# Hashing two more head pairs with GpSimd products and VectorE sums instead of TensorE matmuls

## The chip, the core and the metric

The kernel runs on one NeuronCore of a Trainium2 chip. TensorE (PE) multiplies matrices, VectorE (DVE) and ScalarE (ACT) work on tiles, GpSimd (POOL) is a second, slower elementwise engine that cannot read the matmul accumulators (PSUM), and SyncE (SP) has the queue that most transfers are issued from. Every engine works through its own instructions in the order in which they were written; they meet only at semaphores. The metric is the device time of one execution in microseconds.

## The reference

Attention with a hash mask, followed by a gated feed-forward layer. There are 4 batches of 8 heads, 768 tokens, head dimension 64.

```python
q_bits = (einsum('bhsd,dk->bhsk', q, proj) > 0)      # 6 bits for each token
k_bits = (einsum('bhsd,dk->bhsk', k, proj) > 0)
mask   = q_bucket[..., :, None] == k_bucket[..., None, :]
scores = where(mask, scale * q @ k.T, -1e9)
attn   = softmax(scores) @ v                          # [batch, head, token, 64]
x      = attn, heads side by side                     # [3072, 512]
out    = x + sigmoid(x @ w_res) * ((gelu(x @ w_gate) * (x @ w_val)) @ w_out)
```

The kernel does not build a mask. It appends the six bits, as +0.5 or -0.5, to each token's 64 values of q and k (with one constant column), so that the score matmul itself falls far below the others unless all six bits agree.

## The kernel before

Heads are taken in pairs: 16 pairs, 4 in a batch (batch 0 has pairs 0 to 3, batch 1 has 4 to 7, batch 2 has 8 to 11, batch 3 has 12 to 15). For each batch there are two stages.

The attention stage has 36 slots, nine for each pair. A slot is one call of `scores` (L542, two banks of scores, then one exponential on ScalarE, L553) and, two slots behind, one call of `values` (L515, the products with v). Between them `mlp_mm` issues a few steps of the output projection of the batch before (`project`: L598 for the residual gate, L614 for the product with `w_out`, L617 and L621 on VectorE to finish), so that TensorE never runs dry. A counter spreads these steps: `HELD` = 16 of them are kept for the end of the stage, in the last batch `HELD_LAST` = 20. Each head's accumulator `av` is opened by a memset (L482), preset by a small matmul (L490), copied over its token tiles by VectorE (L494), accumulated into, and normalised (L466, L467). The normalised tokens are turned by a transfer (L470) into `x_sb`.

The gate/value stage has 12 steps (`gate_val`): eight matmuls with `w_gate` and eight with `w_val` (L566), GELU on ScalarE (L583), a product on VectorE (L586). The first three quarters of step 0 (`begun`) are issued ahead, while the last pair's tokens are still being turned.

Before a pair can be attended to, its q and its k must each be loaded (L108), cast into one of four `nat` tiles (L223 for q, L225 for k), hashed, its bits written beside the cast values, and the tile turned by a transfer (L372) into `aug`. There are two ways of hashing:

- By TensorE: VectorE transposes the load (`tr`, L265, into one of six `t32` buffers), 16 matmuls take two pairs at once (`hash_mm`, L283), VectorE transposes the result (`hash_tok`, L303) and writes the bits with four instructions for each of q and k (`bits`, L319).
- By GpSimd and VectorE: for each of the six bits GpSimd multiplies the load with one row of the projection, copied to all partitions (`part`, L357, into one of the same six `t32` buffers), VectorE sums over the 64 values (`part_sum`, L361), and one instruction writes the bits (`bits_sum`, L365). The projection rows come by a transfer (`rows`, L349) and are rearranged by GpSimd (`rows_turned`, L353).

The order of all this is written out by hand. `at(s, ...)` puts work behind slot s, `gv(b, m, ...)` behind step m of batch b's gate/value stage. Batch 1's pairs are all hashed by TensorE in batch 0's stages. For batches 2 and 3 the first two pairs (`xs`) are loaded and transposed in the attention stage of the batch before and hashed by TensorE beside gate step 0, and the last two (`ys`) are hashed by products and sums, whose places `PROD` and `SUMS` count steps: 0 to 11 are steps of the gate/value stage, 12 and up are slots of the next attention stage. GpSimd also casts v and sums it (`vals_a` L432, `vals_s` L440 to L444) for each pair.

Of the kernel before, what the change touches and what calls it, by code (L numbers as in the profile page):

```python
# [46 lines left out]
def kernel(  # L47
# [12 lines left out]
    nc = tc.nc  # L60
    B, H, S, D = q.shape
    NBITS = proj.shape[1]
# [4 lines left out]
    KF = DFF // P  # L67
# [37 lines left out]
    def load(p, side, eng=None):  # L105
        b, hp = divmod(p, HP)
        s = ld_pool.tile([P, HT, D], FP32, tag=f"ld{side}", name=f"ld{side}")
        (eng or nc.sync).dma_start(  # L108
            s.rearrange("p (h t) d -> p h (t d)", h=2),
            (q, k)[side][b, 2 * hp:2 * hp + 2].rearrange("h (p t) d -> p h (t d)", t=T))  # L110
        raw[p, side] = s
# [90 lines left out]
    for s in range(3):  # L202
        n = KF // 3
# [57 lines left out]
    def tr(p, side, h0=0, h1=2):  # L261
        if (p, side) not in t32:
            t32[p, side] = t32_pool.tile([P, HT, 2, 32], FP32, tag="t32", name="t32")
        sl = slice(h0 * T, h1 * T)
        nc.vector.transpose(t32[p, side][:, sl].rearrange("p c h n -> p (c h n)"),  # L265
                            raw[p, side][:, sl].rearrange("p c d -> p (c d)"))
# [80 lines left out]
    def rows():  # L347
        pn = o_pool.tile([P, DMODEL], FP32, tag="o", name="pn")[:, 0:D * NBITS]
        nc.sync.dma_start(pn, proj.rearrange("d n -> (d n)").unsqueeze(0).to_broadcast([P, D * NBITS]))  # L349
        return pn  # L350

    def rows_turned(pn):
        nc.gpsimd.tensor_copy(prow, pn.rearrange("p (d n) -> p n d", n=NBITS))  # L353

    def part(x, j):
        pd = t32_pool.tile([P, HT, D], FP32, tag="t32", name="pd")
        nc.gpsimd.tensor_mul(pd, raw[x], prow[:, j].unsqueeze(1).to_broadcast([P, HT, D]))  # L357
        hparts[x, j] = pd

    def part_sum(x, j):  # L360
        nc.vector.tensor_reduce(stripes(hsum6)[:, :, :, j],  # L361
                                hparts.pop((x, j)).rearrange("p (a c) d -> p a c d", a=3), axis=mybir.AxisListType.X, op=ALU.add)

    def bits_sum(x):
        nc.vector.tensor_scalar(nat_of(x)[:, :, D:D + NBITS].rearrange("p (a c) n -> p a c n", a=3),  # L365
                                stripes(hsum6), 0.0, 0.5,
                                op0=ALU.is_gt, op1=ALU.subtract)

    def turn(p, side):
        x = (p, side)  # L370
        ag = aug_pool.tile([P, HT, P], BF16, tag=f"aug{side}", name=f"aug{side}")
        nc.sync.dma_start_transpose(out=ag, in_=nat_of(x).rearrange("p c n -> p (c n)"))  # L372
        aug[x] = ag
# [184 lines left out]
    gv_work = {}  # L558
# [11 lines left out]
    def gate_val(b, begun, beside=None):  # L570
        for m in range(KF):
            ps = []
            for i, w in enumerate((wg, wv)):
                if m == 0:
                    sp = gv_mm(b, m, w, KM - 1, KM, begun[i])
                else:
                    sp = gv_mm(b, m, w, 0, KM)
                ps.append(sp)
                if m == 0 and i == 1 and beside:
                    beside()  # L580
                if w is wg:
                    gt = g_pool.tile([P, S], BF16, tag="gt", name="gt")
                    nc.scalar.activation(gt, sp[:, 0:S], AF.Gelu)  # L583
            if m == 0 and b > 0:
                hidden[b] = hh_pool.tile([P, KF, S], BF16, tag="hh", name="hh")
            nc.vector.tensor_mul(hidden[b][:, m, :], gt, ps[1][:, 0:S])  # L586
            for piece in gv_work.pop((b, m), []):
                piece()
# [70 lines left out]
    NSLOT = HP * NCH  # L659
    LAST = NPAIR * NCH  # L660
    LAG = 2
    HELD = 16
    HELD_LAST = 20
# [3 lines left out]
    def at(s, *pieces):  # L667
        side_work.setdefault(s, []).extend(pieces)
# [4 lines left out]
    def gv(b, m, *pieces):  # L673
        gv_work.setdefault((b, m), []).extend(pieces)

    def loads(s, *xs):
        for p, what in xs:
            if what == "v":
                at(s, lambda p=p: load_v(p))
            elif p >= NPAIR - 2:  # L680
                for hi in range(2):
                    at(s, lambda p=p, w=what, hi=hi: load_head(p, "qk".index(w), hi, nc.sync))
            else:
                at(s, lambda p=p, w=what: load(p, "qk".index(w)))
# [15 lines left out]
    def tokens(ps, psum=False):  # L700
        hash_tok([(p, side) for p in ps for side in range(2)], psum)
# [67 lines left out]
    begun = []  # L769
# [7 lines left out]
    PROD = (0, 0, 0, 0, 0, 1, 2, 2, 6, 7, 8, 8, 10, 10, 10, 12, 13, 13, 13, 19, 19, 20, 22, 27)  # L777
    SUMS = (1, 2, 2, 4, 4, 6, 7, 8, 9, 10, 10, 11, 12, 12, 13, 17, 19, 21, 21, 23, 23, 29, 30, 31)
    CASTS = (2, 5, 10, 11)
    VALS = (9, 6)  # L780
    LAYS = (0, 0, 3, 5)

    def lay(b, m, x):
        gv(b, m, lambda: bits(*x), lambda: turn(*x))

    for b in range(B - 1):
        s0, p0 = b * NSLOT, (b + 1) * HP
        xs = [(p0 + i, side) for i in range(2) for side in range(2)]
        ys = [(p0 + 2 + i, side) for i in range(2) for side in range(2)]
        if b > 0:  # L790
            for j, (x, y) in enumerate(zip(xs, ys)):
                at(s0 + 24 + 2 * j, lambda x=x: tr(*x))
                at(s0 + 25 + 2 * j, lambda x=x: cast(*x, nc.gpsimd))
                loads(s0 + 2 + 4 * j, (x[0], "qk"[x[1]]))
                loads(s0 + 18 + 3 * j, (y[0], "qk"[y[1]]))
            gv(b, 0, lambda p0=p0: tokens((p0, p0 + 1), True))
            for m, x in zip(LAYS, xs):
                lay(b, m, x)
            for m, y in zip(CASTS, ys):
                gv(b, m, lambda y=y: cast(*y, nc.gpsimd))  # L800
        else:
            for m, names in enumerate(BESIDE):
                for name in names.split():
                    gv(b, m, first.pop(name))
        if b >= FROM:
            s1 = s0 + NSLOT

            def put(n, piece):
                if n < 0:
                    at(s1 + n, piece)  # L810
                elif n < KF:
                    gv(b, n, piece)
                else:
                    at(s1 + n - KF, piece)

            plan = []
            for i, (y, j) in enumerate((y, j) for y in ys for j in range(NBITS)):
                plan.append((PROD[i] + .3, lambda y=y, j=j: part(y, j)))
                plan.append((SUMS[i] + .2, lambda y=y, j=j: part_sum(y, j)))
                if j == NBITS - 1:  # L820
                    plan.append((SUMS[i] + .2, lambda y=y: (bits_sum(y), turn(*y))))
            for n, piece in sorted(plan, key=lambda e: e[0]):
                put(int(n // 1), piece)
    for p in range(HP, NPAIR):
# [7 lines left out]
    NMM = T * (KM + KF)  # L832

    def mlp_mm(n):
        while mlp and n > 0:
            try:
                next(mlp[0])
                n -= 1
                done[0] += 1
            except StopIteration:  # L840
                mlp.pop(0)

    pn = []
    gv(0, 9, lambda: pn.append(rows()))
    gv(0, 11, lambda: rows_turned(pn[0]))
    gate_val(0, begun)
    mlp.append(project(0))
    for s in range(NSLOT, LAST):
        p, c = divmod(s, NCH)
        b, slot = divmod(s, NSLOT)  # L850
        cur = scores(p, c)
        for piece in side_pe.pop(s, []):
            piece()
        held_back = (HELD_LAST - HELD) * (b == B - 1) * max(0, slot - 12) // (NSLOT - 1 - 12)
        mlp_mm(AHEAD + (slot + 1) * (NMM - HELD - AHEAD) // NSLOT - held_back - done[0])
        pending.append(cur)
        while len(pending) > LAG:
            values(*pending.pop(0))
        for piece in side_work.pop(s, []):
            piece()  # L860
        if slot == NSLOT - 1:
            values(*pending.pop(0))
            ps = (HP * (b + 1), HP * (b + 1) + 1)
            mlp_mm(4)
            flush()
            begun = [gv_mm(b, 0, w, 0, KM - 1) for w in (wg, wv)]
            if b < B - 1:
                mlp_mm(NMM)
                gate_val(b, begun, lambda: hashed(ps))
            else:  # L870
                mlp_mm(HELD_LAST - 10)
                gv(b, 0, lambda: mlp_mm(NMM))
                gate_val(b, begun, lambda: mlp_mm(3))
            done[0] = 0
            mlp.append(project(b))
    assert not side_pe and not side_work and not gv_work
# [32 lines left out]
```

## Time and profile before

| | |
|---|---|
| Median of 3 runs | 339.99 us (339.33 to 340.06) |
| Profiled execution | 339.88 us, of which the profile's span is 338.2 us |
| TensorE | busy 330.4 us (98%) |
| VectorE | busy 216.2 us (64%) |
| ScalarE | busy 205.8 us (61%) |
| GpSimd | busy 171.7 us (51%) |

The profile is one execution as the chip's profiler recorded it. A row of a timeline gives the start and the length in us, the engine, the line of the kernel, the operation, the tile written and the tiles read, the shape, how many were merged, and in brackets how long the engine sat idle before it and what released it. A row of a tile or line view gives count and shortest/median/longest duration in ns. A row of a table by stretches gives, for a stretch of the span, its length and the busy us (and number of instructions) of TensorE's matmuls, TensorE's weight loads, VectorE, ScalarE and GpSimd, then the granted TensorE clock, the share of the transfer engines in use, and GB/s. A row of waits gives who was waited for, the us in total and the number of times.

### The profile page before, as it was taken

The page shows a single profiled execution, that of the slowest core. Times are in us where ns is not written, and L with a number is a line of the kernel's source. Part 1 is how long each engine was busy: PE and PEld are TensorE (multiplying, and loading weights), DVE is VectorE, ACT ScalarE, POOL GpSimd, SP SyncE. Part 2 cuts the span into 40 slices and gives each one's busy share as a digit, 9 for nine tenths or more (in the row PEclk, how much of TensorE's full clock was granted, in tenths as well). Part 3 has the DMA queues.
Part 4 walks back from the last instruction along what each step waited for, and adds up shares of the span by engine and source line. Part 5 has one row for each costly group of instructions (what it writes and reads, how often), then busy time and mean ns, then how long its engine had stood idle before and what let it go on. Part 6 is the DMA issues. An engine that isn't in the chain of part 4 may idle for free.

```text
span 338.2 us, 7541 instructions
## 1 busy us (share of the span) xinstructions
PE 330.4 (98%) x3005; PEld 202.7 (60%) x3052; DVE 216.2 (64%) x417; ACT 205.8 (61%) x231; POOL 171.7 (51%) x220
## 2 busy tenths in 40 slices
PE   8999999999999999999999999999999999999995
PEld 4667766555666665665666665666566665666444
DVE  5889457657344847878897765887897434343343
ACT  3899962327999962225999982233999984223220
POOL 6877920801657105998999703998998000000000
PEclk9999999999999999999999999999999999999999
DMA  7989999997985733550487832551251432000012
GB/s 228 378 136 266 215 198 175 175 167 126 209 193 159 237 101 77 95 96 0 105 223 219 251 113 75 96 105 34 48 141 45 99 56 56 31 0 2 31 62 96
DMA packets 72323, 43.29 MB, mean 128 GB/s; under 512 B 50400, under 2 KB 69344, under 8 KB 72288
## 3 DMA queue, kind: packets, MB, share of 16 engines
q1 hardware_dynamic: 65872, 37.56, 43.9%
q0 software_dynamic: 6336, 5.24, 10.5%
q8 instruction: 24, 0.39, 0.5%
q14 instruction: 11, 0.09, 0.1%
q10 hardware_dynamic: 80, 0.00, 0.0%
HBM read 29.56 MB, written 6.29 MB: 106 GB/s over the span
## 4 chain that ended last, share of the span: by engine, by line
PE 95%; DVE 2%; issue 1%; ACT 0%; DVEq 0%
PE sp L566 36%; PE sp L542 19%; PE fps L614 18%; PE av L515 10%; PE rps L598 6%; PE hs L283 2%; PE pt L384 2%; PE wps L189 1%; PE hs L330 1%; DVE hh L586 1%; DVE o L621 1%; DVE fps L617 0%; PE av L487 0%; DVE nat L319 0%; DVE hs L336 0%
## 5 line engine op out<-in xcount | busy, mean ns | idle before, releaser
L553 ACT ACTIVATE e<-sp 128x1024 bf16<-128x1024 f32 x108 | 108.7, 1028 | 7.8 <-PE sp L542 2.8
L357 POOL TENSOR_TENSOR pd<-ld,prow 128x768 f32<-128x768 f32 x48 | 86.1, 1817 | 38.3 <-PE hs L283 34.8
L583 ACT ACTIVATE gt<-sp 128x768 bf16<-128x768 f32 x48 | 38.9, 810 | 89.2 <-PE sp L566 89.2
L542 PE MATMUL sp<-aug,aug 71*128 71x256 bf16 (+1 forms) x384 | 85.8, 325 | 0.0
L614 PE MATMUL fps<-wo,hh 128*128 128x512 bf16 (+2 forms) x289 | 75.0, 361 | 1.3
L586 DVE TENSOR_TENSOR hh<-gt,sp 128x768 bf16<-128x768 bf16 x48 | 45.8, 954 | 40.8 <-PE sp L566 35.1
L566 PE MATMUL sp<-x_sb,wv 128*128 128x256 bf16 (+1 forms) x376 | 70.5, 325 | 0.6 <-DVE hh L586 0.2
L566 PE MATMUL sp<-x_sb,wg 128*128 128x256 bf16 (+1 forms) x376 | 70.5, 325 | 0.5
L515 PEld LDWEIGHTS <-e 128*128 128x128 bf16 x864 | 40.2, 97 | 25.0
L566 PEld LDWEIGHTS <-wv 128*128 128x128 bf16 x384 | 37.5, 98 | 25.1 <-issue 0.4
L566 PEld LDWEIGHTS <-wg 128*128 128x128 bf16 x384 | 37.0, 98 | 25.7 <-issue 1.5
L361 DVE TENSOR_REDUCE hsum<-pd 128x12 f32<-128x768 f32 x48 | 44.2, 942 | 0.4
L515 PE MATMUL av<-va,e 128*128 128x65 bf16 x864 | 43.4, 193 | 0.1
L614 PEld LDWEIGHTS <-hh 128*128 128x128 bf16 x312 | 28.3, 97 | 22.0
L553 ACT ACTIVATE hh<-sp 128x1024 bf16<-128x1024 f32 x36 | 34.7, 1026 | 3.2 <-PE sp L542 2.9
L542 PEld LDWEIGHTS <-aug 71*128 71x128 bf16 x384 | 29.2, 97 | 10.4 <-issue 1.1
L617 DVE SCALAR_TENSOR_TENSOR fps<-th,fps 128x512 f32<-128x512 f32 (+2 forms) x26 | 16.9, 649 | 25.6 <-PE fps L614 25.1
L602 ACT ACTIVATE th<-rps 128x512 f32<-128x512 f32 x24 | 14.3, 594 | 21.3 <-PE rps L598 21.3
L494 DVE COPY av<-av 128x390 f32<-128x390 f32 x24 | 13.7, 571 | 19.0 <-PE av L490 19.0
L598 PE MATMUL rps<-wr,x_sb 128*128 128x512 bf16 x88 | 25.2, 378 | 0.3
L265 DVE STREAM_TRANSPOSE t<-ld 128x768 f32<-128x768 f32 (+1 forms) x24 | 22.1, 926 | 0.1
L223 POOL TENSOR_SCALAR nat<-ld 128x768 bf16<-128x768 f32 (+1 forms) x16 | 13.0, 815 | 16.3 <-issue 15.7
(77 smaller groups left out, 258.9 us busy)
## 6 DMA issues: line engine op xcount, KB each, us to landing
ldv<-in_v_dram SPq DMA_DIRECT2D x16, 384.0 KB, 4.7
out_dram<-o SPq DMA_DIRECT2D x23, 256.0 KB, 2.2
ld<-in_q_dram SPq DMA_DIRECT2D x13, 384.0 KB, 4.6
ld<-in_k_dram SPq DMA_DIRECT2D x13, 384.0 KB, 5.4
wg<-in_moe_w_gate_dram POOLq DMA_DIRECT2D x4, 384.0 KB, 6.7
wv<-in_moe_w_val_dram POOLq DMA_DIRECT2D x4, 384.0 KB, 8.4
wo<-in_moe_w_out_dram POOLq DMA_DIRECT2D x3, 512.0 KB, 8.1
ld<-in_q_dram SPq DMA_DIRECT2D x6, 192.0 KB, 4.5
```

The costliest lines, as they stand in the source:

```text
L265: nc.vector.transpose(t32[p, side][:, sl].rearrange("p c h n -> p (c h n)"), raw[p, side][:, sl].rearrange("p c d -> p (c d)"))
L357: nc.gpsimd.tensor_mul(pd, raw[x], prow[:, j].unsqueeze(1).to_broadcast([P, HT, D]))
L361: nc.vector.tensor_reduce(stripes(hsum6)[:, :, :, j], hparts.pop((x, j)).rearrange("p (a c) d -> p a c d", a=3), axis=mybir.AxisListType.X ...
L515: nc.tensor.matmul(av[p, hi][:, qt, :], e[:, off:off + P], va[:, hi, jt, 0:D + 1], start=first, stop=(p >= HP and jt == T - 1), skip_group ...
L542: nc.tensor.matmul(sp[:, off:off + nq * P], ks[0:KA, hi * T + jt, :], qs[0:KA, hi * T + qt0:hi * T + qt0 + nq, :], start=True, stop=True)
L553: nc.scalar.activation(e, sp, AF.Exp, scale=float(ALPHA))
L566: nc.tensor.matmul(sp[:, c0:c1], w[:, kk, bass.ts(m, P)], xs[:, kk, c0:c1], start=(kk == 0), stop=(kk == KM - 1))
L583: nc.scalar.activation(gt, sp[:, 0:S], AF.Gelu)
L586: nc.vector.tensor_mul(hidden[b][:, m, :], gt, ps[1][:, 0:S])
L598: nc.tensor.matmul(rps, x_sb[b][:, kk, t, :], wr[:, kk, :], start=(kk == 0), stop=(kk == KM - 1))
L614: nc.tensor.matmul(fps[:, cs], hh[:, m, bass.ts(t, P)], wo[:, m, cs], start=(m == 0), stop=(m == KF - 1))
L617: nc.vector.scalar_tensor_tensor(fps[:, cs], th[:, cs], 1.0, fps[:, cs], op0=ALU.add, op1=ALU.mult)
```

## The change

A constant `EARLY = 1` names the batch whose attention stage prepares batch 2. For it alone, all four pairs of batch 2 are hashed by products and sums:

- The `tr` transposes, `hash_mm`, `hash_tok` and `bits` of pairs 8 and 9 are left out.
- Their loads, casts, products and sums get places of their own, counted back from the end of batch 1's attention: -1 to -36 are its slots, -37 and below are steps of batch 0's gate/value stage. The first load and products stand in that stage, most of the rest in the attention stage, the last three sums in steps 1 to 3 of batch 1's gate/value stage.
- Pairs 10 and 11 get a new list of places (`PROD1`, `SUMS1`), later than `PROD` and `SUMS`.
- `rows` and `rows_turned` move from steps 9 and 11 of batch 0's gate/value stage to steps 2 and 4.
- Batch 1 takes over batch 3's way of holding 20 projection steps back and issuing them around gate step 0, where the hash matmuls stood.

```diff
+    EARLY = 1
+    XLOADS = (-45, -42, -38, -28)
+    XCASTS = (-34, -31, -17, 0)
+    XPROD = (-43, -41, -39, -36, -36, -36, -36, -30, -29, -24, -24, -23, -21, -21, -19, -18, -16, -16, -14, -10, -6, -3, -3, -3)
+    XSUMS = (-40, -40, -34, -33, -31, -28, -23, -23, -22, -21, -19, -19, -16, -14, -10, -10, -10, -9, -4, -3, -3, 1, 2, 3)
+    PROD1 = (-1, 3, 4, 4, 5, 7, 7, 7, 7, 8, 8, 11, 13, 14, 14, 18, 18, 18, 20, 22, 23, 24, 24, 27)
+    SUMS1 = (4, 5, 6, 6, 7, 8, 9, 9, 12, 13, 15, 16, 16, 16, 19, 19, 21, 22, 25, 26, 29, 29, 29, 31)
+    CASTS1 = (3, 3, 4, 10)
...
             for j, (x, y) in enumerate(zip(xs, ys)):
+                loads(s0 + 18 + 3 * j, (y[0], "qk"[y[1]]))
+                if b == EARLY:
+                    continue
                 at(s0 + 24 + 2 * j, lambda x=x: tr(*x))
                 at(s0 + 25 + 2 * j, lambda x=x: cast(*x, nc.gpsimd))
                 loads(s0 + 2 + 4 * j, (x[0], "qk"[x[1]]))
-                loads(s0 + 18 + 3 * j, (y[0], "qk"[y[1]]))
...
             def put(n, piece):
-                if n < 0:
+                if n < -NSLOT:
+                    gv(b - 1, n + NSLOT + KF, piece)
+                elif n < 0:
                     at(s1 + n, piece)
...
+            if b == EARLY:
+                for n, m, x in zip(XLOADS, XCASTS, xs):
+                    put(n, lambda x=x: load(*x))
+                    plan.append((m + .1, lambda x=x: cast(*x, nc.gpsimd)))
+                lot(xs, XPROD, XSUMS)
+                lot(ys, PROD1, SUMS1)
+            else:
+                lot(ys, PROD, SUMS)
...
-    gv(0, 9, lambda: pn.append(rows()))
-    gv(0, 11, lambda: rows_turned(pn[0]))
+    gv(0, 2, lambda: pn.append(rows()))
+    gv(0, 4, lambda: rows_turned(pn[0]))
...
-        held_back = (HELD_LAST - HELD) * (b == B - 1) * max(0, slot - 12) // (NSLOT - 1 - 12)
+        held_back = (HELD_LAST - HELD) * (b in (EARLY, B - 1)) * max(0, slot - 12) // (NSLOT - 1 - 12)
...
-            if b < B - 1:
+            if b in (EARLY, B - 1):
+                mlp_mm(HELD_LAST - 10)
+                gv_work.setdefault((b, 0), []).insert(0, lambda: mlp_mm(NMM))
+                gate_val(b, begun, lambda: mlp_mm(3))
+            else:
                 mlp_mm(NMM)
                 gate_val(b, begun, lambda: hashed(ps))
```

More of the change, by code (lines that the diff above doesn't have):

```diff
@@ L794 @@
                 loads(s0 + 2 + 4 * j, (x[0], "qk"[x[1]]))
-                loads(s0 + 18 + 3 * j, (y[0], "qk"[y[1]]))
[L796 to L799, printed above, removed]
+            if b != EARLY:
+                gv(b, 0, lambda p0=p0: tokens((p0, p0 + 1), True))
+                for m, x in zip(LAYS, xs):
+                    lay(b, m, x)
+            for m, y in zip(CASTS1 if b == EARLY else CASTS, ys):
                 gv(b, m, lambda y=y: cast(*y, nc.gpsimd))
@@ L816, with lot @@
             plan = []
[L817 to L821, printed above, removed]
+            def lot(jobs, prod, sums):
+                for i, (y, j) in enumerate((y, j) for y in jobs for j in range(NBITS)):
+                    plan.append((prod[i] + .3, lambda y=y, j=j: part(y, j)))
+                    plan.append((sums[i] + .2, lambda y=y, j=j: part_sum(y, j)))
+                    if j == NBITS - 1:
+                        plan.append((sums[i] + .2, lambda y=y: (bits_sum(y), turn(*y))))
+            if b == EARLY:
[6 more added lines that the diff above has]
+                lot(ys, PROD, SUMS)
             for n, piece in sorted(plan, key=lambda e: e[0]):
@@ L866 @@
             begun = [gv_mm(b, 0, w, 0, KM - 1) for w in (wg, wv)]
-            if b < B - 1:
+            if b in (EARLY, B - 1):
[3 more added lines that the diff above has]
+            else:
                 mlp_mm(NMM)
                 gate_val(b, begun, lambda: hashed(ps))
[L870 to L873, printed above, removed]
             done[0] = 0
```

## The prediction

> **What bounds the kernel now.** First the page's 40 slices and the chain that ended last, then a table by stage.
>
> ```profile
> POOL 6877920801657105998999703998998000000000
> PE 95%; DVE 2%; issue 1%; ACT 0%; DVEq 0%
> ```
>
> TensorE carries 95% of the chain: what it issues is the time, and another engine costs something only where TensorE comes to wait for it. GpSimd (POOL) has its empty slices around 44 to 107 us, which is where the change puts work.
>
> ```profile
> core 0: us, PE busy (x) PEld busy (x) DVE busy (x) ACT busy (x) POOL busy (x), PEclk, DMA share, GB/s
> 80.50:123.50 43.00, 42.50 (x471) 26.47 (x478) 22.75 (x49) 39.24 (x43) 18.54 (x31) 1.00 0.74 181
> 123.50:158.80 35.30, 35.04 (x236) 20.78 (x238) 25.99 (x45) 11.80 (x15) 26.74 (x18) 1.00 0.37 77
> 158.80:201.70 42.90, 42.40 (x470) 26.46 (x477) 33.60 (x62) 39.28 (x43) 33.11 (x39) 1.00 0.67 178
> 237.00:279.00 42.00, 41.50 (x463) 26.05 (x471) 28.26 (x54) 38.93 (x42) 23.77 (x27) 1.00 0.36 78
> 279.00:313.70 34.70, 34.49 (x212) 20.39 (x213) 13.85 (x17) 11.60 (x14) 0.00 (x0) 1.00 0.07 22
> ```
>
> The rows are attention of batch 1 and its gate/value stage, attention of batch 2, then attention and gate/value stage of batch 3. In each TensorE is busy within 0.5 us of the stage. Batch 1 takes 78.3 us; batch 3, in whose gate/value stage nothing is hashed, takes 76.7. The granted clock is 1.00. VectorE's (DVE's) busy time goes from 22.75 us in the first attention stage to 33.60 in the second, and the stage gets no longer: VectorE has room.
>
> **Part 1: the hash matmuls go.** This is the end of batch 1's attention on TensorE, and the same place in batch 3, whose schedule batch 1 now takes.
>
> ```profile
> 128.76 1.51 PE L283 MATMUL hs<-t,projw 128*32 128x192 f32 x32
> 130.20 1.48 PE L566 MATMUL sp<-x_sb,wg 128*128 128x512 bf16 x8
> ```
>
> From 128.76 to 130.20 TensorE does nothing but the hash: 1.44 us, in line with nothing beside it. The build has 16 such matmuls fewer (two records each). The stage table prices the same thing a second way: 78.3 - 76.7 = 1.6 us. I take 1.44, the row of the thing itself. The held-back output projection (20 steps instead of 16 left for the gate/value stage) only moves TensorE work: its four steps leave attention (43.0 to about 42.1) and come back behind gate step 0. ScalarE then has 39.2 us in 42.1; batch 3 does 38.93 in 42.0, so that costs nothing.
>
> **Part 2: work taken off and put on VectorE and GpSimd.**
>
> ```profile
> 130.49 0.59 DVE L303 STREAM_TRANSPOSE htp<-hs 128x384 f32<-128x384 f32 x1
> 131.11 1.91 DVE L319 TENSOR_SCALAR nat<-htp 32x72 bf16<-32x72 f32 x8
> L265 DVE STREAM_TRANSPOSE t<-ld 128x768 f32<-128x768 f32 x4 | 3.8, 955 | 0.0
> L361 DVE TENSOR_REDUCE hsum<-pd x48: 896/945/956, 134.0 to 260.7; 128x12 f32<-128x768 f32 x48
> 160.93 0.23 DVE L365 TENSOR_SCALAR nat<-hsum 128x72 bf16<-128x72 f32 x1
> L357 POOL TENSOR_TENSOR pd<-ld,prow x48: 1804/1817/1834, 107.9 to 256.5; 128x768 f32<-128x768 f32 x48
> 130.33 7.12 POOL L357 TENSOR_TENSOR pd<-ld,prow 128x768 f32<-128x768 f32 x4 [18.81 <-PE hs L283]
> ```
>
> Off VectorE: 4 transposes 3.8, one token transpose 0.59, 16 bit writes 2 x 1.91; 8.2 us. Onto it: 24 sums x 0.945 + 4 x 0.23 = 23.6 us. Onto GpSimd: 24 products, back to back 7.12 / 4 = 1.78 each, 42.7 us. In the build's order 2 of the new sums stand in gate/value stage 0, 19 in attention 1 and 3 in stage 1; of the later 24 (pairs 10, 11), 8 stand in stage 1 and 16 in attention 2. Attention 1 then has 22.75 - 3.8 + 19 x 0.945 + 3 x 0.23 = 37.6 us of VectorE in 42.1. None of it is TensorE's, so it is priced at nothing as long as three covers hold.
>
> **Cover A: the eviction copies.** Each head's accumulator is preset by TensorE, copied by VectorE (L494), then accumulated into two steps later for a pair's first head, one step later for its second. Sums queued ahead of the copy delay it.
>
> ```profile
> 98.03 0.56 DVE L494 COPY av<-av 128x390 f32<-128x390 f32 x1
> 99.39 0.56 DVE L467 TENSOR_TENSOR x_tok<-av,rec 128x384 bf16<-128x384 f32 x1
> 101.97 0.57 DVE L494 COPY av<-av 128x390 f32<-128x390 f32 x1 [1.83 <-PE av L490]
> 104.43 0.41 PE L515 MATMUL av<-va,e 128*128 128x65 bf16 x8
> 107.78 0.57 DVE L494 COPY av<-av 128x390 f32<-128x390 f32 x1 [0.64 <-PE av L490]
> 109.12 0.41 PE L515 MATMUL av<-va,e 128*128 128x65 bf16 x8
> ```
>
> The copy at 101.97 may end 1.9 us later (104.43); the one at 107.78, a second head, 0.95 (the second half of the step at 109.12). The worst place in the new order is the first: behind the copy that ends at 98.59 stand a sum (to 99.5), the normalisation (0.8, to 100.3), a sum, a memset and two sums (to 103.2), 0.23, and the copy: it ends at 104.0, with 0.4 us to spare. Of the others in attention 1 none is closer. In attention 2:
>
> ```profile
> 80.50:104.40 23.90, 23.62 (x249) 14.49 (x252) 10.14 (x25) 22.40 (x25) 11.58 (x22) 1.00 0.92 204
> 158.80:182.70 23.90, 23.62 (x250) 14.54 (x253) 20.08 (x37) 22.53 (x25) 23.43 (x26) 1.00 0.67 179
> ```
>
> With VectorE at 20.08 instead of 10.14 us of 23.9, TensorE does the same 23.62. The change adds three sums to the second stretch (16 for 13): 22.9 of 23.9. Bounds for what that costs: nothing (this pair of rows) to 1.0 us (22.9 being full within the 1.0 that is left, and all of that met as one wait). I take 0.1, because the row nearest to it, 84% busy, shows nothing.
>
> **Cover B: GpSimd in time.** A sum whose product is late stops VectorE's queue, evictions included.
>
> ```profile
> 66.41 1.63 POOL L225 CAST nat<-ld 128x768 bf16<-128x768 f32 x2
> 83.50 0.87 POOL L353 COPY prow<-pn 128x384 f32<-128x384 f32 x1 [15.47 <-DMA pn<-in_proj_dram]
> 84.35 0.99 POOL L440 TENSOR_TENSOR v<-ldv 128x384 f32<-128x384 f32 x1
> 87.21 1.00 POOL L440 TENSOR_TENSOR v<-ldv 128x384 f32<-128x384 f32 x1
> 182.68 0.94 DVE L361 TENSOR_REDUCE hsum<-pd 128x12 f32<-128x768 f32 x1
>   POOL pd L357: 3.2, 4
> 71.39 0.95 DVE L586 TENSOR_TENSOR hh<-gt,sp 128x768 bf16<-128x768 bf16 x1 [0.76 <-PE sp L566]
> 58.19 0.84 SPq L116 DMA_DIRECT2D ldv<-in_v_dram  x1
> pn<-in_proj_dram SPq DMA_DIRECT2D x1, 192.0 KB, 4.9
> DMA to landing us min/median/max: 2.6/4.7/9.2
> ```
>
> GpSimd is free of weight loads at 66.41. The projection rows now go into SyncE's queue ahead of the transfer at 58.19; with the 4.9 us that they took to land (the row "pn") they are there by 64, and the first load, issued next, by about 68 if it takes the longest that a q or k load took (9.2 us, the last row). The first two products end near 69 and 71; their sums stand behind the gate product at 71.39, so nothing waits. From there to the last product of pair 11: 0.85 + 48 products x 1.78 + 10 casts x 0.8 + 6 value pairs x 2.86 (84.35 to 87.21) = 111.5 us, to 177.9. Its sum is due at 182.68 - 1.44 = 181.2: 3.3 us free, against 3.2 us that GpSimd waited before for product buffers (the row "POOL pd L357"). So the last product comes about when it is due. In SyncE's queue the row transfer and the first three transfers (0.84 us or so each to issue) pass ahead of the turns of pairs 4 to 7, which are needed from 80.5 on and are some 3 us later for it at 60; in attention 1 the new turns wait there for their bits, with output stores and token turns behind them whose VectorE work stands behind the same bits. Nothing.
>
> **Cover C: the last token turn of batch 1.** Gate step 0's last quarter needs it, and batch 3's schedule leaves less work in front.
>
> ```profile
> 119.96 0.56 DVE L467 TENSOR_TENSOR x_tok<-av,rec 128x384 bf16<-128x384 f32 x1
> 123.68 0.20 DVE L466 RECIPROCAL rec<-av 128x6 f32<-128x6 f32 x1
> 279.46 0.56 DVE L467 TENSOR_TENSOR x_tok<-av,rec 128x384 bf16<-128x384 f32 x1
> 283.14 0.49 PE L566 MATMUL sp<-x_sb,wg 128*128 128x512 bf16 x2
> DMA to landing us min/median/max: 2.7/2.9/5.2
> ```
>
> 280.02 + 2.9 = 282.9, so 0.2 us is left in batch 3, and in batch 1 a memset, two sums and a copy, 0.11 + 1.89 + 0.57 = 2.6 us, now stand between the last two normalisations, where 123.68 - 120.52 = 3.2 us lie (3.0 in the shortened stage): they fit. Cost nothing, up to 1 us if the product there is late.
>
> **The sum.** -1.44 + 0.1 = -1.3 on the profiled execution: its span 338.2 becomes 336.9 and its 339.88 us 338.5; the median of the runs, 339.99, lies 0.1 above it: 338.6.
>
> **Rivals.**
> 1. Late products (slower). Buffer waits double with the number of products: 6.4 instead of 3.2, so the last product comes 3.1 us late, and the copies behind its sum have 0.95 of slack: TensorE waits 2.2 us, 340.8. It decides from 1.44 + 0.95 = 2.4 us of lateness on. For it: 3.3 us of room is little over 115. Against: the long waits of before (18.81 us in the row of part 2) were for hash matmuls, not for sums. Chance 0.22.
> 2. The gain is eaten: several small waits at covers A and C, together 0.8 to 2.1 us, leave 339.3 to 340.6. For it: margins of 0.2 and 0.4 us. Against: the 84% row. Chance 0.18.
> 3. Products and sums shut each other out. The 48 products last 1804 to 1834 ns with sums running beside most of them, a spread of 30 ns, so this hardly happens. If each new product lost half a sum, 24 x 0.47 = 11 us, GpSimd would be some 11 us late and the time near 349. Chance 0.02. The Trainium skill, Perfetto Trace Analysis, Optimizing Scalar/DVE Operations, warns that moving work between GpSimd and VectorE might not help since they share an SBUF read port; by that warning this rival is the outcome, but the trace's 30 ns disagree for reductions.
>
> **How the numbers follow.** Forecast 0.58. 0.2% is 0.68 us, about what runs can tell from no change. Forecast and a little of rival 2 make faster 0.60; the rest of 2 and the mildest of 1, 0.16 within 0.2%; 0.24 slower. The likeliest case alone reaches from 338.2 (1.6 and no waits, less 0.2 of scatter) to 339.2; the range goes up to rival 1's time with a little scatter: 338.2 to 341.0.
>
> **What would show it.** Right: no hash between steps 0 and 1 of stage 1, batch 1 at 76.8 us, products without pause from 67 us on, sums waiting under 1 us in all, TensorE's waits under 0.3. Wrong: TensorE idle ahead of L515 or L490 released by L494 or L482, idle ahead of L566 for the token turn at the start of stage 1, scores of pair 11 waiting for their turn, or VectorE idle released by L357 with evictions behind.

## The result and the profile after

The changed kernel is slower: 345.21 us in the median (344.48 to 346.29) against 340.0 (339.33 to 340.11), a ratio of 1.016 [1.0135, 1.0185]. A second set of runs gave 343.78 us (343.49 to 344.67), 1.0121 [1.0102, 1.014]. The forecast was 338.6, with a range up to 341.0. The profiled execution took 346.29 us with a span of 344.6, 6.4 us more than the span before.

All of it lies in one stage. From the first score of batch 1's attention to its first gate matmul it is now 80.20 to 130.30, 50.1 us instead of 43.0; the gate/value stage behind it takes 34.7 instead of 35.3. From the page, GpSimd's slices, the granted clock and the chain that ended last:

```profile
POOL 6876910926999999979999930998999000000000
PEclk9999999999999989999999999999999999999999
PE 79%; POOL 13%; issue 3%; DVE 2%; DMA 1%; ACT 0%; POOLq 0%; DVEq 0%
```

TensorE carried 95% of the chain before and carries 79% now; GpSimd carries 13%, in a kernel in which it was to cost nothing. The waits between 80 and 131 us (total, times, longest) say who waited for it:

```profile
POOL nat L225 <- DMA aug<-nat: 8.8, 1, 8.8
DVE hsum L361 <- POOL pd L357: 7.5, 8, 2.5
PE av L515 <- POOL pd L357: 2.3, 1, 2.3
PE av L515 <- POOL va L433: 2.1, 1, 2.1
```

VectorE waits for products 8 times and TensorE twice for more than 2 us. But the first row stands at the head: GpSimd itself waited 8.8 us, once, for a transfer. Its timeline around that place:

```profile
67.12 3.58 POOL L357 TENSOR_TENSOR pd<-ld,prow 128x768 f32<-128x768 f32 x2
70.64 0.82 POOL L225 CAST nat<-ld 128x768 bf16<-128x768 f32 x1
80.29 0.83 POOL L225 CAST nat<-ld 128x768 bf16<-128x768 f32 x1 [8.83 <-DMA aug<-nat]
81.08 8.89 POOL L357 TENSOR_TENSOR pd<-ld,prow 128x768 f32<-128x768 f32 x5
```

The cast at 80.29 is that of pair 7's k (`cs71`, step 9 of batch 0's gate/value stage). There are four `nat` tiles, and this one was last written for pair 5's k, so the cast must wait until the turn of pair 5's k (`tu51`) has read it. Product 3 stands behind the cast in GpSimd's queue. SyncE's queue shows why the turn is late (the last row of this view is GpSimd's, the loads of `w_out`). The turn's own rows (issue time in ns, start, then landing in us) come second, and the same of before third:

```profile
57.81 0.90 SPq L349 DMA_DIRECT2D pn<-in_proj_dram  x1
58.76 0.44 SPq L108 DMA_DIRECT2D ld<-in_q_dram  x1
59.24 0.47 SPq L116 DMA_DIRECT2D ldv<-in_v_dram  x1
59.80 0.41 SPq L108 DMA_DIRECT2D ld<-in_k_dram  x1
60.32 22.51 SPq L372 DMA_TRANSPOSE aug<-nat  x5
63.83 2.33 POOL L208 DMA_DIRECT2D wo<-in_moe_w_out_dram  x3
```

```profile
L372 SPq DMA_TRANSPOSE aug<-nat x1: 5193/5193/5193, 64.8 to 64.8; - x1
DMA to landing us min/median/max: 15.5/15.5/15.5
```

```profile
L372 SPq DMA_TRANSPOSE aug<-nat x1: 1742/1742/1742, 62.0 to 62.0; - x1
DMA to landing us min/median/max: 4.0/4.0/4.0
```

Before, the turn was issued at 62.0, ahead of the three loads of `w_out` that GpSimd issues from about 64, and landed at 66.0, 1.2 us ahead of the cast that waits for it (the second of the two that start at 66.41). Now it is issued 2.8 us later, beside those loads (512 KB each), and lands at 80.3. The chain from there to TensorE: TensorE's timeline first, then what stands behind each of its two waits, on VectorE and on GpSimd:

```profile
107.92 0.42 PE L515 MATMUL av<-va,e 128*128 128x65 bf16 x8 [2.31 <-POOL pd L357]
120.53 0.40 PE L515 MATMUL av<-va,e 128*128 128x65 bf16 x8 [2.12 <-POOL va L433]
```

```profile
106.17 0.95 DVE L361 TENSOR_REDUCE hsum<-pd 128x12 f32<-128x768 f32 x1 [1.62 <-POOL pd L357]
107.30 0.56 DVE L494 COPY av<-av 128x390 f32<-128x390 f32 x1
```

```profile
116.05 3.58 POOL L357 TENSOR_TENSOR pd<-ld,prow 128x768 f32<-128x768 f32 x2
119.57 0.82 POOL L432 CAST va<-ldv 128x768 bf16<-128x768 f32 x1
```

The first waits for an accumulator copy (L494, 107.30 to 107.86) that stands on VectorE behind a sum whose product was late. The second waits for GpSimd's cast of pair 7's v, which stands behind products in GpSimd's own queue.

### The profile page after: what moved, and what is told of

Its sections match the earlier page's. It is cut to its first block, busy times and chain, and to the rows that moved or that the text cites. A ratio compares the mean times of both kernels' runs of the same rounds, so it can differ in the third digit from the quotient of the medians.

```text
span 344.6 us, 7552 instructions
## 1 busy us (share of the span) xinstructions
PE 333.7 (97%) x3020; PEld 202.0 (59%) x3020; DVE 229.9 (67%) x424; ACT 206.1 (60%) x231; POOL 214.0 (62%) x244
## 4 chain that ended last, share of the span: by engine, by line
PE 79%; POOL 13%; issue 3%; DVE 2%; DMA 1%; ACT 0%; POOLq 0%; DVEq 0%
PE sp L566 30%; PE sp L542 15%; PE fps L614 14%; POOL pd L357 9%; PE av L515 8%; PE rps L598 5%; PE hs L283 2%; PE pt L384 2%; DMA x_sb<-x_tok 1%; PE wps L189 1%; POOL v L440 1%; PE hs L330 1%; POOL nat L225 1%; POOL va L432 1%; DVE hh L586 1%
## 5 line engine op out<-in xcount | busy, mean ns | idle before, releaser
L357 POOL TENSOR_TENSOR pd<-ld,prow 128x768 f32<-128x768 f32 x72 | 128.8, 1810 | 18.1 <-DVE hh L586 13.5
L614 PE MATMUL fps<-wo,hh 128*128 128x512 bf16 (+2 forms) x312 | 79.8, 363 | 0.0
L586 DVE TENSOR_TENSOR hh<-gt,sp 128x768 bf16<-128x768 bf16 x48 | 45.8, 955 | 45.1 <-PE sp L566 35.2
L361 DVE TENSOR_REDUCE hsum<-pd 128x12 f32<-128x768 f32 x72 | 66.3, 940 | 8.1 <-POOL pd L357 7.8
L566 PE MATMUL sp<-x_sb,wg 128*128 128x512 bf16 (+1 forms) x384 | 70.9, 326 | 0.2
L566 PE MATMUL sp<-x_sb,wv 128*128 128x512 bf16 (+1 forms) x384 | 70.9, 326 | 0.2 <-DVE hh L586 0.2
L553 ACT ACTIVATE hh<-sp 128x1024 bf16<-128x1024 f32 x36 | 34.7, 1026 | 3.2 <-PE sp L542 2.9
L602 ACT ACTIVATE th<-rps 128x512 f32<-128x512 f32 x24 | 14.3, 594 | 24.1 <-PE rps L598 24.1
L598 PE MATMUL rps<-wr,x_sb 128*128 128x512 bf16 x96 | 28.1, 387 | 0.0
L494 DVE COPY av<-av 128x390 f32<-128x390 f32 x24 | 13.6, 567 | 11.4 <-PE av L490 11.4
L225 POOL CAST nat<-ld 128x768 bf16<-128x768 f32 (+1 forms) x16 | 12.9, 804 | 11.5 <-DMA aug<-nat 8.8
```

What stands on the lines that cost most here:

```text
L225: eng.tensor_copy(dst, raw[x][:, sl])
L361: nc.vector.tensor_reduce(stripes(hsum6)[:, :, :, j], hparts.pop((x, j)).rearrange("p (a c) d -> p a c d", a=3), axis=mybir.AxisListType.X ...
L553: nc.scalar.activation(e, sp, AF.Exp, scale=float(ALPHA))
L566: nc.tensor.matmul(sp[:, c0:c1], w[:, kk, bass.ts(m, P)], xs[:, kk, c0:c1], start=(kk == 0), stop=(kk == KM - 1))
L598: nc.tensor.matmul(rps, x_sb[b][:, kk, t, :], wr[:, kk, :], start=(kk == 0), stop=(kk == KM - 1))
L614: nc.tensor.matmul(fps[:, cs], hh[:, m, bass.ts(t, P)], wo[:, m, cs], start=(m == 0), stop=(m == KF - 1))
```

## The experiments

The theory: the late turn holds the cast, the cast holds all later products, and the lateness reaches TensorE through copies and value casts. Its rival: products and sums simply don't fit into batch 1's attention (VectorE or GpSimd too full), and the late cast only comes on top. Times are medians, ratios are to the kernel before with 95% intervals.

| kernel | us | ratio |
|---|---|---|
| changed kernel, last cast after the stage | 338.38 (337.98 to 339.12) | 0.9953 [0.9941, 0.9965] |
| changed kernel, two turns first | 338.61 (338.01 to 339.46) | 0.996 [0.9944, 0.9976] |
| both | 338.36 (338.15 to 338.48) | 0.9954 [0.9935, 0.9973] |
| kernel before, moved transfers only | 339.45 (339.24 to 340.23) | 0.9991 [0.9982, 1.0] |
| changed kernel without the early products | 338.81 (338.38 to 339.75) | 0.9974 [0.9963, 0.9985] |
| changed kernel, `w_out` earlier | 340.89 (340.44 to 342.04) | 1.0031 [1.0018, 1.0044] |
| changed kernel, `w_out` later | 338.83 (338.2 to 339.47) | 0.9961 [0.9949, 0.9974] |
| last cast after the stage, 1 product more | 339.34 (338.76 to 340.26) | 0.9984 [0.9971, 0.9997] |
| the same, 2 products more | 343.28 (342.81 to 343.53) | 1.01 [1.0082, 1.0118] |
| the same, 4 products more | 346.76 (345.59 to 347.23) | 1.0199 [1.0176, 1.0222] |

**The last cast after the stage.** The cast of pair 7's k and its turn leave the gate/value stage and stand at slot 1 of the attention stage, behind products 3 to 7 and the first sums of pair 4's v. The transfers stay as they are in the changed kernel.

```diff
-    "tu51 cs71 h30 h31 h32 h33 tk3 bt60 bt61 tu60",
-    "tu61 bt70 bt71 tu71",
+    "tu51 h30 h31 h32 h33 tk3 bt60 bt61 tu60",
+    "tu61 bt70 bt71",
...
+            at(NSLOT + 1, first.pop("cs71"), first.pop("tu71"))
```

> Only the cast of pair 7's k (and its turn) moves behind the products that GpSimd has for slot 0, so that nothing stands behind its wait for pair 5's turn; the loads stay where the change put them and the turn may land as late as it did (80 us). Late-turn theory: GpSimd's 8.8 us of idleness goes, the product of the tightest place is there 8 us earlier, VectorE waits for products under 1.5 us in all instead of 7.8, TensorE's idle places of 2.3 and 2.1 us in attention 1 go with the dip of its clock, and the time is 338.4 to 339.3. Full-VectorE theory (19 sums in that stage are too many, the wait only shows it): GpSimd no longer waits but evictions still stand behind sums, TensorE still loses 2 us or more there, and the time is 341 to 344.

Measured 338.38 us, 0.9953 [0.9941, 0.9965]: faster than both kernels. The turn is as late as ever (issued 64.8, landed 14.2 later), but nothing waits for it. GpSimd's timeline:

```profile
72.92 8.89 POOL L357 TENSOR_TENSOR pd<-ld,prow 128x768 f32<-128x768 f32 x5 [1.53 <-DVE hsum L361]
83.82 0.82 POOL L225 CAST nat<-ld 128x768 bf16<-128x768 f32 x1
```

Products 3 to 7 start 8.2 us earlier than in the changed kernel, and VectorE's waits for products in the whole span fall to this row:

```profile
DVE hsum L361 <- POOL pd L357: 0.3, 2, 0.2
```

All 24 products and sums are still there, so the rival falls: they fit. The table by stretches shows what their lateness had cost, the changed kernel first, then this one:

```profile
80.00:130.00 50.00, 44.43 (x468) 26.47 (x466) 35.07 (x66) 39.70 (x42) 49.08 (x48) 0.97 0.77 165
```

```profile
80.00:130.00 50.00, 50.00 (x518) 30.36 (x517) 37.58 (x71) 41.90 (x46) 49.37 (x51) 1.00 0.75 170
```

TensorE is idle for 5.6 us of the 50 in one and for nothing in the other. VectorE is busier in the faster kernel.

**Two turns first.** The turns of pair 4's and pair 5's k go ahead of the projection rows and the moved loads.

```diff
-    "tu50 cs70 bt51",
-    "vs4 bt41 tr70 cs60",
+    "tu50 cs70 bt51 tu51",
+    "vs4 bt41 tu41 tr70 cs60",
...
-    "tu41 cs61",
-    "tu51 cs71 h30 h31 h32 h33 tk3 bt60 bt61 tu60",
+    "cs61",
+    "cs71 h30 h31 h32 h33 tk3 bt60 bt61 tu60",
...
-    gv(0, 2, lambda: pn.append(rows()))
+    gv(0, 3, lambda: pn.append(rows()))
```

> The turns of pair 5's and pair 4's k are issued ahead of the moved loads and the row transfer, everything else as in the change. Late-turn theory with the moved loads as its cause: the turn of pair 5 lands about 62 instead of 80, the cast does not wait, the first products start 2 to 4 us later than in the change (near 69 to 71) because their load now follows the turns, and the time is 338.6 to 339.8. If the weight loads of w_out that GpSimd issues at 64 us hold the turn back, and not the moved loads, then the turn still lands in time here, since it is issued before them. Full-VectorE theory: 341 to 344.

Measured 338.61, 0.996 [0.9944, 0.9976]. The two turns are issued at 57.7 and 59.5 and land 4.1 us later; the cast waits for nothing. Mending the cause does the same as taking away the one who waits for it.

**Moved transfers only.** The kernel before, with the rows and the loads of pairs 8 and 9 at the changed kernel's places and nothing else.

```diff
-                loads(s0 + 2 + 4 * j, (x[0], "qk"[x[1]]))
+                if b == 1:
+                    piece = lambda x=x: load(*x)
+                    at(s0 + 8, piece) if j == 3 else gv(0, (3, 6, 10)[j], piece)
+                else:
+                    loads(s0 + 2 + 4 * j, (x[0], "qk"[x[1]]))
...
-    gv(0, 9, lambda: pn.append(rows()))
-    gv(0, 11, lambda: rows_turned(pn[0]))
+    gv(0, 2, lambda: pn.append(rows()))
+    gv(0, 4, lambda: rows_turned(pn[0]))
```

> The kernel before with one part of the change alone: the row transfer and the loads of pairs 8 and 9 at the change's places, the hash still by TensorE. Late-turn theory: the turn of pair 5's k lands 10 us or more late again and GpSimd's cast of pair 7's k waits some 9 us, but GpSimd has nothing urgent behind it, so the time stays within 0.5 us of 340.0. If the late turn also costs something by itself (scores waiting for it), it is over 341.

Measured 339.45, 0.9991 [0.9982, 1.0], 0.55 us below 340.0, where 0.5 at most was expected. GpSimd's cast waits even longer here:

```profile
79.30 0.83 POOL L225 CAST nat<-ld 128x768 bf16<-128x768 f32 x1 [9.48 <-DMA aug<-nat]
```

The moved transfers make the wait, and the wait costs nothing while GpSimd has nothing behind the cast that anyone needs.

**Without the early products.** The changed kernel without the 24 products, 24 sums and 4 bit writes of pairs 8 and 9. Their hash is left out of the computation, so this prices the change without its new work.

```diff
-                lot(xs, XPROD, XSUMS)
+                for n, x in zip((-28, -19, -9, 3), xs):
+                    plan.append((n + .2, lambda x=x: turn(*x)))
```

> The change without the 24 products, 24 sums and 4 bit writes of pairs 8 and 9, which are left out of the computation; the casts, turns, loads and the held-back projection steps stay. It measures what the removed matmuls are worth if the new hash costs nothing. Priced from the trace of before: 1.44 us less than before, 338.4 to 338.8. A time near 340 would say that the removed hash matmuls bought nothing; a time near 345 that the cost is in the moved loads and the projection, and not in the products and sums. The cast of pair 7's k still waits for its late turn here, with nothing urgent behind it.

Measured 338.81, 0.9974 [0.9963, 0.9985]; the cast waits 8.4 us here too. It is no faster than the versions that do the products, so 24 products and 24 sums that are on time cost nothing that these runs can tell.

**Which transfers hold the turn.** First the loads of `w_out` were moved ahead, behind the loads of the gate weights; then behind the first two products, right ahead of the last cast.

```diff
-    "cs40 h23 tk2 bt50",
+    "cs40 w9 w10 w11 h23 tk2 bt50",
...
-    "w9 w10 w11 tr60",
+    "tr60",
```

> The changed kernel, but GpSimd issues the three loads of the output weights (512 KB each) before step 0's casts, some 10 us earlier than now (63.8), so that they are through before the turn of pair 5's k is issued at 64.8. Theory A, the four loads that SyncE issues between 57.8 and 60.2 hold the turn: it still lands 12 to 16 us after its issue, the cast of pair 7's k still waits 6 to 9 us, time 344 to 346. Theory B, the output weights' loads hold it (they are issued 63.8 to 66.1, just around that turn): it lands by 70, the cast waits under 2 us, time 338.4 to 339.5. Both together: the wait is halved, 340 to 343.

Measured 340.89, 1.0031 [1.0018, 1.0044]. The time lies in the band that was given for both theories together, but for a reason that none of them named. The three loads, issued from 44 to 47, take 15.0 to 19.8 us to land, and now the turns of pair 4's and pair 5's q, with no moved load ahead of them, are the late ones. SyncE's row of the first, then GpSimd's cast behind the second (the row names no releaser; it starts when that turn, issued at 59.7, has landed 8.2 us later):

```profile
L372 SPq DMA_TRANSPOSE aug<-nat x1: 4424/4424/4424, 55.1 to 55.1; - x1
DMA to landing us min/median/max: 11.4/11.4/11.4
```

```profile
68.03 0.82 POOL L223 TENSOR_SCALAR nat<-ld 128x768 bf16<-128x768 f32 x1 [20.39 <-issue]
```

So large weight loads under way hold a turn by themselves. The time is lost elsewhere than in the changed kernel: the late cast holds the first two products, their sums hold the gate products on VectorE (L586), and TensorE waits for these 1.02 and 0.68 us (at 78.10 and 81.54). The later position of the same loads:

```diff
-    "w9 w10 w11 tr60",
+    "tr60",
...
-    "tu51 cs71 h30 h31 h32 h33 tk3 bt60 bt61 tu60",
+    "tu51 w9 w10 w11 cs71 h30 h31 h32 h33 tk3 bt60 bt61 tu60",
```

> The changed kernel with the three loads of the output weights issued by GpSimd after products 1 and 2, right ahead of the last cast (about 70.5), so that no such load is under way while the turns of pair 4's and pair 5's k are issued (60.3, 64.8). If SyncE's moved loads hold the turn by themselves, it lands at 75 to 80 and the cast waits 5 us or more: 342 to 345. If the output weights' loads hold it, it lands by 70 and the cast waits under 1 us: 338.4 to 339.5, to which up to 1 us comes if the output weights themselves come late for their first matmul (81.4 in the held-back version).

Measured 338.83, 0.9961 [0.9949, 0.9974]. The turn of pair 5's k and, below it, GpSimd's timeline:

```profile
L372 SPq DMA_TRANSPOSE aug<-nat x1: 2651/2651/2651, 65.6 to 65.6; - x1
DMA to landing us min/median/max: 5.9/5.9/5.9
```

```profile
69.70 2.33 POOL L208 DMA_DIRECT2D wo<-in_moe_w_out_dram  x3
71.99 0.87 POOL L225 CAST nat<-ld 128x768 bf16<-128x768 f32 x1
```

The turn is issued behind the same four transfers as in the changed kernel and lands after 5.9 us instead of 15.5. The `w_out` loads made 9.6 us of the delay. The moved transfers made the rest: the turn ahead of this one still took 4.7 us to issue and landed after 7.8, against 1.9 and 4.4 before the change. By moving 2.8 us of SyncE's queue the change pushed the turn from ahead of the weights to beside them.

**How much lateness the stage bears.** In the version with the last cast held back, one product (bit 2 of pair 8's q) is issued two, three or five times with the same result, which makes every later product late.

```diff
-        nc.gpsimd.tensor_mul(pd, raw[x], prow[:, j].unsqueeze(1).to_broadcast([P, HT, D]))
+        for _ in range(3 if (x, j) == ((2 * HP, 0), 2) else 1):
+            nc.gpsimd.tensor_mul(pd, raw[x], prow[:, j].unsqueeze(1).to_broadcast([P, HT, D]))
```

> The held-back version with that product issued twice: some 1.8 to 2.4 us of lateness. The runs with 3.6 and 7.1 us lost 4.9 and 8.4 us, more than one for one, so the slack is small and a TensorE wait of about 2 us costs granted clock besides. If the products stand right at the edge already, this costs 1.8 to 2.6 us: 340.2 to 341. If there are 1 to 2 us of slack and the loss grows in a step once a value cast or a bit copy comes late, 338.4 to 339.2, with no idle time of TensorE over 0.3 us.

> The version with the last cast held back until after the stage, in which one product of pair 8's q is issued three times (the same result written anew), so that all later products come two products, some 3.6 us, later. The forecast on record held that GpSimd has 3.3 us free and that lateness decides from about 2.4 us: by that this costs 0 to 1.2 us against the held-back version's 338.4, that is 338.4 to 339.6. If attention 1 has no such slack and each microsecond on GpSimd is one on the span, 342.

> As the run before, with that product issued five times: some 7.1 us of lateness, near the 8.8 us that the changed kernel's cast waits. If lateness of the products alone explains the loss, whatever made them late, this costs 4 to 5.5 us beyond the held-back version: 342.5 to 344, with idle time of TensorE in front of the value sums and behind products as in the changed kernel. If the loss comes from the late turn itself or from the busier transfers, and not from the products, the time stays under 340.

The lateness is read from GpSimd's cast of pair 7's v, which stands behind these products: how long after GpSimd's cast at about 60 us it starts, against the same in the version with the last cast held back. It is 1.8, 3.7 and 7.5 us, and the losses against 338.38 are 0.96, 4.90 and 8.38 us. In the changed kernel the lateness counted this way is 7.2 us and the loss 6.8; in its second profile 6.2 and (by that set's median) 5.4. Lateness of GpSimd's products alone, with no late transfer that they wait for, makes losses that rise with it in the same order, and with four products more TensorE waits for the same two, 2.31 and 2.12 us.

The third expectation named the places that were found, but all three times missed: 339.34 lies between the two bands that were given, 343.28 above both, 346.76 above the 344 at which the band for lateness alone ended. The forecast's 0 to 1.2 us for two extra products fell. A microsecond of lateness beyond the slack costs more than one: with two products more TensorE waits 2.4 us, 1.7 us of granted clock are missing behind the longer wait, and the span is 4.8 us longer.

The slack is about 1 us. In the version with the last cast held back, GpSimd's cast of pair 7's v and the TensorE rows that need it:

```profile
112.25 0.82 POOL L432 CAST va<-ldv 128x768 bf16<-128x768 f32 x1
113.02 0.15 POOL L433 MEMSET va<- 128x12 bf16 x1
```

```profile
114.17 0.41 PE L515 MATMUL av<-va,e 128*128 128x65 bf16 x8
```

It is ready at 113.17 and read at 114.17. One product more makes TensorE wait there, two products more make it wait longer (TensorE's timelines, where the lines of the kernel are one higher):

```profile
115.43 0.40 PE L516 MATMUL av<-va,e 128*128 128x65 bf16 x8 [0.71 <-POOL va L434]
```

```profile
117.55 0.40 PE L516 MATMUL av<-va,e 128*128 128x65 bf16 x8 [2.12 <-POOL va L434]
```

**The changed kernel again, and both mends.**

> The changed kernel once more, unaltered, for a second profile. The time is expected between 344.4 and 346.4 as before, the cast of pair 7's k to wait 8 to 9 us again. If the granted clock of 0.61 between 120 and 124 us is what parts 346.2 from 344.5, a profiled execution near 344.5 shows no such dip; if it shows one as well, the difference comes from elsewhere.

The second set gave 343.78 us, a little below the expected band. The cast waited 7.8 us instead of 8.8, and the second TensorE wait was 0.49 us instead of 2.12: how late the turn lands differs from run to run, and so does the time. That this is why the runs of the changed kernel spread from 343.5 to 346.3 was not tested. The dip of the clock (0.50 for some 3 us, shown in the last section) came here too, behind the first wait instead of the second, so it is not what parts the two.

> The turns of pairs 4 and 5 issued ahead of the moved loads, and the last cast held back as well. Each alone gave 338.4 to 338.6. If the late turn was the only cost, the two do the same and don't add: 338.2 to 338.7. If the turns' traffic delays anything else that counts, up to 0.5 us less: 337.9.

338.36 us, 0.9954 [0.9935, 0.9973]: the two mends don't add, as expected of one cause. The best versions are 1.6 us below the kernel before and 6.8 below the changed one.

## Why the prediction was wrong

**The step that failed** is the last part of cover B: the transfers that "pass ahead of the turns of pairs 4 to 7, which are needed from 80.5 on", priced at "Nothing". It counted the scores as the only readers of a turn. A turn also frees the `nat` tile, and a cast waited for that on GpSimd's queue with product 3 behind it. It waited 8.8 us, and the kernel lost 6.8 us against the version in which nothing stands behind that wait. The sign that the prediction named for this came: VectorE idle, released by L357, with evictions behind. The same part priced GpSimd's casts at 0.8 us each, by their duration, with no wait in front. It also took "some 3 us later" for the turn, which is right for its issue (2.8) but not for its landing (14.3 us later), since it didn't ask what else would be under way by then.

**GpSimd's room, 3.3 us, was mis-sized as well**: 1.0 measured. It was taken at the last product's sum, and there it was about right (181.2 was the time it is due, and in the version with the last cast held back it starts at 181.04, after waiting 0.16 us for its product); but the cast of pair 7's v, in the same queue, has less room.

**Part 1 and the sum hold.** The mended versions, which do all that the change does, give 338.36 to 338.83 us, within the 338.2 to 339.2 of the likeliest case. Batch 1 takes 76.8 us in the version with the last cast held back (80.12 to 156.93), as the prediction named it. The gain of 1.6 us [1.2, 2.0] for the version with the last cast held back lies around the 1.44 and 1.6 of part 1.

**Cover A holds.** With 19 sums in the stage TensorE waits for no copy when the products are on time: taken 0.1, measured nothing. **Cover C holds**: the wait for the last token turn was 0.3 us in the version with the last cast held back, against 0 taken and 1 as bound.

**The rivals.** Rival 1, late products, is what happened, with another cause: buffer waits rose to 5.2 us in the version with the last cast held back (3.2 before), not 6.4, and cost nothing. Its price of 2.2 us and its threshold of 2.4 were too mild, since the slack was 1 us and the lateness 7. Rival 2 (margins at A and C) did not happen. Rival 3 did not happen: products in the changed kernel take 1810 ns on average in the page, with sums beside them.

## What to carry to other kernels

When transfers are moved ahead in a queue, list for each one pushed back every reader of its end: who reads what it writes, and who may overwrite what it reads. A wait that was harmless at the end of an engine's work becomes the bound once work is put behind it in that in-order queue; the kernel with moved transfers only waited 9.5 us and lost nothing. A transfer's landing is no constant: look which loads will be under way at its new time, and move whichever of the two has room.

## What the runs showed of the hardware

**A turn beside large loads takes up to nearly four times as long.** Issue rose from 1.74 to 5.19 us and landing from 4.0 to 15.5, behind four loads of its own queue and beside three that another engine issued. With GpSimd's loads under way and none of the four ahead, another turn took 4.42 and 11.4; with the four ahead and GpSimd's loads moved away, this one took 2.65 and 5.9. The Trainium skill, DMA: Bandwidth & Descriptors, Issuing engines are not separate DMA queues, says that transfers of all issuing engines share the same 16 DMA engines and interleave. These traces agree: GpSimd's loads of `w_out`, moved away, gave SyncE's turn 9.6 us back.

**A TensorE wait of 2 us can be followed by half the granted clock for some 3 us.** The table by stretches of 1 us in the changed kernel, behind the wait that ends at 120.53 (the clock is the third number from the end):

```profile
120.00:121.00 1.00, 0.47 (x9) 0.34 (x9) 0.94 (x3) 0.00 (x0) 1.00 (x3) 0.93 0.07 25
121.00:122.00 1.00, 1.00 (x4) 0.34 (x3) 0.99 (x2) 0.16 (x1) 1.00 (x1) 0.50 0.00 0
122.00:123.00 1.00, 1.00 (x12) 0.86 (x11) 0.95 (x3) 0.86 (x1) 1.00 (x2) 0.50 0.83 158
123.00:124.00 1.00, 1.00 (x4) 0.30 (x2) 0.02 (x1) 0.44 (x1) 1.00 (x2) 0.50 1.15 206
124.00:125.00 1.00, 1.00 (x14) 0.75 (x13) 0.00 (x0) 1.00 (x2) 0.92 (x2) 0.86 2.79 174
```

The clock that is missing is 0.07 + 3 x 0.50 + 0.14 = 1.7 us, which at 0.50 is a dip of 3.4 us. With the 5.6 us of idle time that makes 7.3 of the 7.9 us between the spans of the changed kernel (344.6) and of the version with the last cast held back (336.7). The wait of 2.31 us at 107.92 was followed by no dip; in the second profile, the wait of the same length there was. With two and with four products more, the wait of 2.12 us was followed by a dip as well (0.74, 0.50, 0.50 and 0.55 from 118 to 122 us with two), and with four the wait of 2.31 us was not. The Trainium skill, TensorE: Matmul & The Clock Gate, What's actually happening, gives two states, full and half, and an idle window of about 3.4 us that runs freely. The 0.50 and the length agree; that 3.4 us idle are needed does not, since 2.1 us were enough here. Why one wait is followed by a dip and another isn't stays open.
